# Attention blocks of six, five and five key tiles, with 27 exponential tiles and twelve slots for moving operands

## The chip, the cores and the metric

The kernel runs on one core of a Trainium2 chip. The metric is the device time of one execution in microseconds (us). Its engines work side by side, each through its own queue in order: TensorE (PE, with its weight loads as PEld), VectorE (DVE), ScalarE (ACT), GpSimd (POOL) and SyncE (SP, which issues all DMAs here).

## What is computed

Two independent results stand side by side in the output of 2048 x 2048 values, all in float32. The left half is multi-head attention with 32 heads of width 32 over 2048 rows; the right half is the real part of a two-dimensional Fourier transform, as products with given matrices.

```python
qkv = (x @ wqkv).reshape(B, S, 3, H, Dh)            # S = 2048, D = 1024, H = 32, Dh = 32
scores = einsum("bhqd,bhkd->bhqk", q, k) * Dh ** -0.5
p = softmax(scores, axis=-1)
left = einsum("bhqk,bhkd->bhqd", p, v).reshape(B, S, D) @ wo

a = einsum("bsd,ed->bse", xb, dft_hid_re);  b = einsum("bsd,ed->bse", xb, dft_hid_im)
right = dft_seq_re @ a - dft_seq_im @ b
```

## The kernel before

**Dense products.** The projection to Q, K and V (`qkv`), the two stages of the transform (`dense1`, `dense2`) and the output projection (`project`) are products of large matrices. Each is done as seven products of quarter matrices and sums of quarters instead of eight products, so each stage goes through seven steps (`ORDER`; `STEPS` in `qkv`, where they are split into twelve). Float32 accuracy comes from splitting every operand into a high and a low part and adding three matmuls, so a term of `group` (line 347) is three matmuls of 128x512 at line 357, 12 or 24 of them to a group. These are called fills: 6720 in all, in a fixed order.

**Operands.** A stationary operand (`piece`, line 452) has three buffers for each half. A moving operand (`moving`, line 478) is fetched through a ring of raw tiles (`fetch`, line 383: DMAs, and sums at line 421), then split by `halves` (line 435): a cast to the high part (line 443 on DVE, line 441 on ACT where `spare` allows), and a subtraction for the low part (line 446, on POOL or DVE). The two halves go into one numbered slot of 4 KB for each partition. A step uses eight moving operands, and each slot's split waits until the last fill that used the slot's former content is done. `load_x`, `load_b` and `load_ab` put the operands of even steps into one set of eight slots and those of odd steps into another; the loads of the next step are queued while the step runs, about one after each group. Other slots hold the running sums of the steps (`accs`), and slots 24 to 27 are made in a pool that takes the place of the attention's tiles when these are released (`op_pool`).

**Attention.** For each head three streams of PE work are written out. S (line 1148): scores of 128 query rows against 1024 keys in a PSUM tile `psS` (two buffers), whose maximum DVE takes (line 1154) and whose exponentials ACT sums (line 1157). T (line 1271): the scores transposed, 128 keys by 512 query columns in `psT` (two buffers), shifted by the maxima; ACT writes their exponentials into a tile `pt` (line 1275), of which there are `NPT` = 19. V: after every `PVB` = 4 key tiles, that is 16 `pt` tiles, one block of products with V (line 1289). These use the array as four groups of 32 columns, one for each 512 query columns:

```python
for k, j, box, _, _ in todo:
    nc.tensor.matmul(
        po["p"][j * DH : j * DH + DH, :], VT[h][:, k, :], box["t"], start=(k == t + 1 - PVB), stop=(k == t),
        tile_position=(0, j * DH),
    )
v = op("PE", SWITCH + PVB * PV, pv, [load[t // PVB], *(x[3] for x in todo)], [vuse, *(x[4] for x in todo)])
```

The block's sum leaves PSUM by a copy (line 1300) or an addition (line 1302) on DVE. In the trace each of these V matmuls in plain float32 has two records.

**The order.** A planner (`Plan` and the loop from line 1348) plays the program through with costs written by hand (line 305) and so fixes the order of every engine when the program is built. PE takes S and T as ACT and DVE need them, V blocks when they are ready, and fills in between. Fills are paced by `nf / (FILL - RES) <= done / ATT` (line 1401), where `done` is the planned cost of the attention work begun and `ATT` its total.

**The end.** `behind` (line 1010) is called at the last step (13) of `dense2`: from there raw tiles come from the pool that replaces the attention's, gated by the stores of all heads' results (`over`), and casts may go to ACT (`spare`). `project` loads its first operands through the earlier ring (line 1079), the others through the new one.

Of the kernel before, what the change touches and what calls it, by code (L numbers as in the profile page):

```python
# [19 lines left out]
H = 32  # L20
DH = 32
# [3 lines left out]
NPT = 19  # L25
NE = 4
PVB = 4
# [182 lines left out]
def kernel(  # L210
# [94 lines left out]
    MM, PV, SWITCH, TINY = 0.234, 0.762, 0.62, 0.17  # L305
# [17 lines left out]
    ATT = H * (128 * MM + 16 * PV + 16 / PVB * SWITCH)  # L323
# [41 lines left out]
    slots = [[] for _ in range(28)]  # L365
# [169 lines left out]
    def qkv():  # L535
# [211 lines left out]
        def qk_group(x, W, b, n):  # L747
            p = STEPS[x][0]
            early = x < 5
            h = FIRST.get(p)  # L750
            if p == 1 and n == 0:
                if early:
                    X[2 * b], X[2 * b + 1] = acc(b)
                else:
                    X[2 * b], X[2 * b + 1] = accs(16 + b - PAIRS)
            group(((chunk(W, c), (XS[x, 4 * n + c], whole)) for c in range(4)), 4,
                  gather(p, 2 * b + n, qk_result(b + 8 * h[0], 2 * h[1] + n, early) if h else None, early, None if b % 2 else SCALE))
# [8 lines left out]
        for x, (p, blocks, v) in enumerate(STEPS[:10]):  # L766
            spare[0] = x < 5
            for i, b in enumerate(blocks):
# [8 lines left out]
                if x == 0 and i == 1:  # L777
                    for k in range(4, 8):
                        load_x(0, k)
# [4 lines left out]
                if x == 0:  # L784
                    if i == 1:
                        for c in range(4):
                            load_v_weight(0, c)
                else:
                    for k in range(8 * i // len(blocks), 8 * (i + 1) // len(blocks)):
                        load_x(x + 1, k)  # L790
            for t in range(8 if v else 0):
# [8 lines left out]
            if x == 4:  # L800
                for u in ahead[0].users:
                    att_gate.extend(u)
# [3 lines left out]
        for x in (10, 11):  # L806
            for t in range(8):
                v_group(x, t)
                if x == 10:
                    load_x(11, t)  # L810
                    if t < 4:
                        load_v_weight(11, t)
# [76 lines left out]
    def dense1():  # L889
# [31 lines left out]
        for n in range(8):  # L921
            load_b(0, n)
        X = {}
        for x, p in enumerate(ORDER):
            for i in range(8):
                a = piece(a_terms(p, i), (s1_d[i], s1[i]) if p == 6 else None)
                if p == 1:
                    X[i] = accs(i)
# [7 lines left out]
                if x < 6:  # L936
                    load_b(x + 1, i)
                else:
                    load_ab(0, i)
# [4 lines left out]
    def load_ab(step, k):  # L944
# [11 lines left out]
        AB[step, k] = moving((16 if step % 2 else 8) + k, terms, (t2_d[m][k], t2[m][k]) if p == 6 else None)  # L956

    def dense2():

        y_st = [[[], []] for _ in range(NS)]  # L960
        for m in range(2):
# [13 lines left out]
            for x, p in enumerate(ORDER):  # L975
                step = 7 * m + x
                if step == 13:
                    behind()
                for i in range(8):
                    if p in (1, 7) and i % 2 == 0:  # L980
                        X[p, i // 2] = accs((0 if p == 1 else 4) + i // 2)
# [15 lines left out]
                    if step < 13:  # L997
                        load_ab(step + 1, i)
# [11 lines left out]
    def behind():  # L1010

        over.extend(o for h in o_st for o in h)
        for i in range(24, 28):
# [4 lines left out]
    over, within = [], where[0]  # L1018

    def project():  # L1020
# [15 lines left out]
        def b_terms(p, c):  # L1036
# [11 lines left out]
            1: ([8, 12], 0), 7: ([16, 20], 24), 2: ([0, 16], 12), 6: ([20, 0], 24),  # L1048
            5: ([16, 20], 12), 3: ([0, 16], 24), 4: ([20, 0], 12),
# [29 lines left out]
        tail, where[0] = where[0], within  # L1079
        load_b(1)  # L1080
        load_a(1, J0 + J1)
        where[0] = tail
        for x, p in enumerate(ORDER):
            for i in range(8):
                j, t = divmod(i, 4)
                if p == 1 and i % 2 == 0:
                    X[i // 2] = accs(4 + i // 2)
                if p == 7 and i % 2 == 0:
                    Y[i // 2] = accs(8 + i // 2)
# [168 lines left out]
    def transposed(h):  # L1258
# [4 lines left out]
        for t in range(NS):  # L1263
# [19 lines left out]
            if (t + 1) % PVB == 0:  # L1283
                load, vuse = vts[h]

                def pv(todo=todo, t=t):
                    po["p"] = psD.tile([P, NB], F32, name="pd")
                    for k, j, box, _, _ in todo:
                        nc.tensor.matmul(  # L1289
                            po["p"][j * DH : j * DH + DH, :], VT[h][:, k, :], box["t"], start=(k == t + 1 - PVB), stop=(k == t),  # L1290
# [6 lines left out]
                def gather_o(t=t):  # L1297
                    if t + 1 == PVB:
# [5 lines left out]
                e = op("DVE", EVAC, gather_o, [v] + (oold if t + 1 == PVB else []), [ouse], -1)  # L1304
# [33 lines left out]
    dense2()  # L1338
    project()
# [118 lines left out]
```

## Time and profile before

| | |
|---|---|
| median of three runs | 3033.72 us (3032.64 to 3034.45) |
| profiled execution | 3032.8 us, of which the profile's span is 3031.0 us |
| PE busy | 3004.3 us (99%) |
| DVE busy | 2451.4 us (81%) |
| ACT busy | 2297.5 us (76%) |
| POOL busy | 788.6 us (26%) |
| V matmul records at line 1289 | 4096, first at 268.7 us, last at 2798.3 us |
| TensorE clock granted | 1.000 |

The page of the profile gives busy time by engine, forty slices of the span, the chain of work that ended last, and groups of instructions by line. The timeline lists instructions in order of time, equal ones merged: the start, the length from the first start to the last end, the engine, the line and the tiles. Since matmuls are pipelined, an instruction's length overlaps with the next; what one costs is read from start to start.

### The profile page before, as it was taken

To read this page: it belongs to the slowest core of one execution; us is meant where nothing else is said; L and a number is where in the kernel's file an instruction comes from. 1 tells how busy PE (TensorE), PEld (TensorE's weight loads), DVE (VectorE), ACT (ScalarE), POOL (GpSimd) and SP (SyncE) were. 2 spreads that over 40 slices of the span, in tenths; PEclk is the share of its full clock that TensorE was granted. 3 is DMA by queue.
4 is the path that set the end of the run, shared out by engine and by line. 5 is a ranking of instruction groups with operands and counts; after the bars stand their busy time and mean duration, and the time that the engine had idled before them with its cause. 6 is when DMAs were issued, how large, how long until landed. Compare 5 with 4: busy or idle time off the path is not lost.

```text
span 3031.0 us, 45312 instructions
## 1 busy us (share of the span) xinstructions
PE 3004.3 (99%) x14912; PEld 2142.4 (71%) x14912; DVE 2451.4 (81%) x3303; ACT 2297.5 (76%) x4328; POOL 788.6 (26%) x587
## 2 busy tenths in 40 slices
PE   8999999999999999999999999999999999999999
PEld 7887666666766667666677766676666766666787
DVE  7779888788978878887778888878777888886886
ACT  4347888888888888888888888888888888884321
POOL 2313324222212221221011243332111344221232
PEclk9999999999999999999999999999999999999999
DMA  9975657766635535564534675455433577446942
GB/s 341 351 233 180 192 182 226 222 208 229 227 98 170 175 119 157 156 193 123 156 112 128 198 240 181 147 161 174 132 119 94 167 230 227 150 139 216 372 141 98
DMA packets 376314, 558.07 MB, mean 184 GB/s; under 512 B 110896, under 2 KB 110896, under 8 KB 376016
## 3 DMA queue, kind: packets, MB, share of 16 engines
q1 hardware_dynamic: 376080, 555.17, 57.4%
q8 instruction: 120, 1.97, 0.3%
q14 instruction: 114, 0.93, 0.1%
HBM read 401.93 MB, written 153.09 MB: 183 GB/s over the span
## 4 chain that ended last, share of the span: by engine, by line
PE 90%; DVE 6%; DMA 2%; issue 1%; ACT 1%; SPq 0%; POOL 0%; DVEq 0%; ACTq 0%; POOLq 0%
PE pd L357 39%; PE psT L1271 15%; PE psS L1148 15%; PE pd L1289 15%; PE psT L357 6%; DVE negm L1154 2%; ACT psS L1157 1%; DVE slot L443 1%; DVE h L443 0%; DVE slot L446 0%; DVE l L446 0%; DVE raw L421 0%; DMA er<-in_xa 0%; DVE e L446 0%; DMA raw<-in_wv 0%
## 5 line engine op out<-in xcount | busy, mean ns | idle before, releaser
L1275 ACT ACTIVATE pt<-psT 128x512 f32<-128x512 f32 x2048 | 1167.9, 639 | 352.6 <-PE psT L1271 344.2
L1154 DVE TENSOR_REDUCE negm<-psS 128x1 f32<-128x1024 f32 x1024 | 1237.7, 1220 | 179.8 <-PE psS L1148 173.6
L1157 ACT ACTIVATE psS<-psS,negm 128x1024 f32<-128x1024 f32 x1024 | 1161.1, 1134 | 82.8 <-DVE negm L1154 79.4
L357 PE MATMUL pd<-slot,h 128*128 128x512 f32 x3304 | 1130.7, 394 | 0.1
L1271 PE MATMUL psT<-qs,ks 98*128 98x512 f32 x2048 | 816.5, 403 | 2.0 <-ACT pt L1275 1.5
L357 PEld LDWEIGHTS pd<-slot,h 128*128 128x128 f32 x3304 | 624.8, 189 | 140.7 <-issue 1.7
L357 PE MATMUL pd<-slot,l 128*128 128x512 f32 x1652 | 650.3, 394 | 0.8 <-DVE l L446 0.8
L1271 PEld LDWEIGHTS psT<-qs,ks 98*128 98x128 f32 x2048 | 383.3, 189 | 202.1 <-issue 87.2
L1148 PE MATMUL psS<-ks,qs 96*128 96x512 f32 x1552 | 476.7, 396 | 7.9 <-ACT psS L1157 5.8
L1289 PE MATMUL pd<-pt,vt 128*32 128x512 f32 x4096 | 466.0, 595 | 1.8 <-DVE e L590 0.4
L446 POOL TENSOR_TENSOR l<-raw,h 128x512 fp32r<-128x512 f32 x149 | 199.4, 1338 | 920.8 <-PE psT L1271 425.2
L421 POOL TENSOR_TENSOR raw<-raw,g 128x512 f32<-128x512 f32 x199 | 264.8, 1336 | 504.2 <-DMA raw<-in_ct 115.5
L357 PEld LDWEIGHTS pd<-slot,l 128*128 128x128 f32 x1652 | 312.5, 189 | 70.6 <-DVE l L446 1.1
L1148 PEld LDWEIGHTS psS<-ks,qs 96*128 96x128 f32 x1552 | 290.0, 189 | 83.2 <-ACT psS L1157 18.2
L1289 PEld LDWEIGHTS pd<-pt,vt 128*32 128x32 f32 x4096 | 120.0, 109 | 276.9 <-issue 256.3
L446 POOL TENSOR_TENSOR slot<-raw,slot 128x512 fp32r<-128x512 f32 x129 | 180.2, 1405 | 360.0 <-DVE slot L443 261.8
L1157 ACT ACTIVATION_READ_ACCUMULATOR psS<-psS,negm 128x1 f32 x1024 | 257.4, 251 | 0.0
L357 PE MATMUL pd<-slot,slot 128*128 128x512 f32 x768 | 195.5, 392 | 0.0
L1302 DVE TENSOR_TENSOR ot<-ot,pd 128x512 f32<-128x512 f32 x96 | 65.9, 687 | 157.6 <-PE pd L1289 157.6
L357 PEld LDWEIGHTS pd<-slot,slot 128*128 128x128 f32 x768 | 144.5, 188 | 31.5
L1148 PE MATMUL psS<-ks,qx 96*128 96x512 f32 x496 | 152.1, 397 | 1.4 <-ACT psS L1157 1.4
L443 DVE CAST h<-raw 128x512 fp32r<-128x512 f32 x305 | 138.8, 457 | 15.9 <-PE pd L357 14.9
(117 smaller groups left out, 2002.2 us busy)
## 6 DMA issues: line engine op xcount, KB each, us to landing
raw<-in_ct SPq DMA_DIRECT2D x224, 256.0 KB
g<-in_ct SPq DMA_DIRECT2D x128, 256.0 KB
qk_d<-e SPq DMA_DIRECT2D x52, 512.0 KB
qs<-qk_d SPq DMA_DIRECT2D x128, 192.0 KB
ks<-qk_d SPq DMA_DIRECT2D x128, 192.0 KB
raw<-ab_d SPq DMA_DIRECT2D x96, 256.0 KB
c<-u_d SPq DMA_DIRECT2D x88, 256.0 KB
g<-ab_d SPq DMA_DIRECT2D x80, 256.0 KB
```

What stands on the lines that cost most here:

```text
L357: nc.tensor.matmul(box["ps"], a[1]((a[0].hi, a[0].lo)[u]()), b[1]((b[0].hi, b[0].lo)[v]()), start=k == 0, stop=k == n - 1)
L421: (nc.gpsimd if e == "POOL" else nc.vector).tensor_tensor(out=dest(), in0=dest() if a is None else a.get(), in1=other["q"] if "q" in other ...
L443: nc.vector.tensor_copy(hi(), raw())
L446: (nc.gpsimd if e == "POOL" else nc.vector).tensor_tensor(out=lo(), in0=raw(), in1=f(hi()), op=ALU.subtract)
L1148: nc.tensor.matmul(p[:, i * NB : i * NB + NB], (qx["t"] if own else QS[h % 2][0:96])[:, qt * P : qt * P + P], KS[h % 2][0:96, c * 1024 + i ...
L1154: nc.vector.tensor_reduce(out=ST["negm"][:, c, qt : qt + 1], in_=box["p"], axis=AX.X, op=ALU.max, negate=True)
L1157: nc.scalar.activation(box["p"], box["p"], AF.Exp, bias=ST["negm"][:, c, qt : qt + 1], accum_out=ST["sums"][:, c, qt : qt + 1])
L1271: nc.tensor.matmul(box["p"], KS[h % 2][0:98, t * P : t * P + P], QS[h % 2][0:98, j * NB : j * NB + NB], start=True, stop=True)
L1275: nc.scalar.activation(box["t"], box["p"], AF.Exp)
L1289: nc.tensor.matmul(po["p"][j * DH : j * DH + DH, :], VT[h][:, k, :], box["t"], start=(k == t + 1 - PVB), stop=(k == t), tile_position=(0, ...
L1302: nc.vector.tensor_tensor(out=po["o"], in0=po["o"], in1=po["p"], op=ALU.add)
```

## The change

- V blocks end after key tiles 6, 11 and 16 of a head (`ENDS`), three for each head instead of four. A block waits for all V tiles up to its last, and for its 24 or 20 exponential tiles.
- `NPT` rises from 19 to 27, which takes 16 KB more of each partition.
- Slots 20 to 23 leave the common pool. Moving operands go round in twelve slots: a step's first four operands are queued during the step before, the last four with the step's own first group. Their slots are those of the first four operands of the step before.
- Sums move to the slots left (`SUMS`), and the V weights of two early steps to slots 28 to 31 in the early pool `vp`; the attention's gate waits for their users too.
- `behind` is called after `dense2`, and the first operands of `project` go through its ring too.
- The planner's costs become `PV` = 0.786 and `SWITCH` = 0.515, with three switches for each head in `ATT`.

```diff
-NPT = 19
+NPT = 27
-PVB = 4
+ENDS = (0, 6, 11, 16)
...
-        if i >= 24:
-            return op_pool().tile(shape, dt, name=f"slot{i}")
+        if i >= 20:
+            return (vp if i >= 28 else op_pool()).tile(shape, dt, name=f"slot{i}")
...
+    AROUND, SUMS = (16, 17, 18, 19, 4, 5, 6, 7, 8, 9, 10, 11), (0, 1, 2, 3, 12, 13, 14, 15)
-    MM, PV, SWITCH, TINY = 0.234, 0.762, 0.62, 0.17
+    MM, PV, SWITCH, TINY = 0.234, 0.786, 0.515, 0.17
-    ATT = H * (128 * MM + 16 * PV + 16 / PVB * SWITCH)
+    ATT = H * (128 * MM + 16 * PV + 3 * SWITCH)
...
-            XS[x, k] = moving(8 * ((x + 1) % 2) + k, x_terms(p, k, x >= 5), (tx_d[k], tx[k]) if x == 3 else (t1x_d[k], t1x[k]) if x == 2 else None)
+            if x < 5:
+                i = 8 * ((x + 1) % 2) + k
+            else:
+                i = (8 * (x - 5) + k) % 12 if x < 11 or k < 4 else 8 + k
+            XS[x, k] = moving(i, x_terms(p, k, x >= 5), (tx_d[k], tx[k]) if x == 3 else (t1x_d[k], t1x[k]) if x == 2 else None)
-            WV[x, c] = moving((20 if x in (1, 3, 10) else 16) + c, w_terms(p, lambda i, j: wv[i, 4 * j + c], sv_d[c], sv[c]), (sv_d[c], sv[c]) if p == 6 else None)
+            WV[x, c] = moving((28 if x in (1, 3) else 12 if x == 10 else 16) + c, w_terms(p, lambda i, j: wv[i, 4 * j + c], sv_d[c], sv[c]), (sv_d[c], sv[c]) if p == 6 else None)
...
-            B[x][n] = moving(16 - 8 * (x % 2) + n, b_terms(p, n), (t1_d[n], t1[n]) if p == 6 else None)
+            B[x][n] = moving(AROUND[(8 * x + n) % 12], b_terms(p, n), (t1_d[n], t1[n]) if p == 6 else None)
+                if i == 0:
+                    for n in range(4, 8):
+                        load_b(x, n)
-                if x < 6:
-                    load_b(x + 1, i)
-                else:
-                    load_ab(0, i)
+                if i % 2:
+                    load_b(x + 1, i // 2) if x < 6 else load_ab(0, i // 2)
...
-        AB[step, k] = moving((16 if step % 2 else 8) + k, terms, (t2_d[m][k], t2[m][k]) if p == 6 else None)
+        AB[step, k] = moving(AROUND[(8 * (7 + step) + k) % 12], terms, (t2_d[m][k], t2[m][k]) if p == 6 else None)
-                if step == 13:
-                    behind()
+                            if i == 0 and k:
+                                for c in range(4, 8):
+                                    load_ab(step, c)
-                    if step < 13:
-                        load_ab(step + 1, i)
+                    if step < 13 and i % 2:
+                        load_ab(step + 1, i // 2)
...
-        for i in range(24, 28):
+        for i in range(20, 28):
-        tail, where[0] = where[0], within
         load_b(1)
         load_a(1, J0 + J1)
-        where[0] = tail
...
-            if (t + 1) % PVB == 0:
+            if t + 1 in ENDS:
+                t0 = ENDS[ENDS.index(t + 1) - 1]
-                v = op("PE", SWITCH + PVB * PV, pv, [load[t // PVB], *(x[3] for x in todo)], [vuse, *(x[4] for x in todo)])
+                v = op("PE", SWITCH + (t + 1 - t0) * PV, pv, [*load[: t // 4 + 1], *(x[3] for x in todo)], [vuse, *(x[4] for x in todo)])
...
     dense2()
+    behind()
     project()
```

More of the change, by code (lines that the diff above doesn't have):

```diff
@@ L364 @@
     RAW, HR, LR, GR, ER = Ring(5), Ring(3), Ring(3), Ring(3), Ring(NE)
-    slots = [[] for _ in range(28)]
+    slots = [[] for _ in range(32)]
     def take_slot(i):
@@ L800, in qkv @@
             if x == 4:
-                for u in ahead[0].users:
+                for u in ahead[0].users + slots[28:]:
                     att_gate.extend(u)
@@ L808, in qkv @@
                 v_group(x, t)
[L809 to L812, printed above, removed]
+                if x == 11 and t < 4:
+                    load_x(11, 4 + t)
+                elif x == 10 and t < 2:
+                    for k in range(2):
+                        load_x(10, 4 + 2 * t + k)
+                elif x == 10 and 2 <= t < 6:
+                    load_x(11, t - 2)
+                    load_v_weight(11, t - 2)
         for b in range(8):
@@ L917, in load_b @@
             p = ORDER[x]
[L918 removed]
+            B[x][n] = moving(AROUND[(8 * x + n) % 12], b_terms(p, n), (t1_d[n], t1[n]) if p == 6 else None)
         B = [[None] * 8 for _ in ORDER]
[L921 removed]
+        for n in range(4):
             load_b(0, n)
@@ L1016, in behind @@
         spare[0] = True
-    over, within = [], where[0]
+    over = []
     def project():
```

32 lines of the change are left out of this document (17 added, 15 removed).

## The prediction

> **What bounds the kernel now.** The page comes first: busy time, the slices with the clock, and the chain that ended last.
>
> ```profile
> span 3031.0 us, 45312 instructions
> ...
> PE 3004.3 (99%) x14912; PEld 2142.4 (71%) x14912; DVE 2451.4 (81%) x3303; ACT 2297.5 (76%) x4328; POOL 788.6 (26%) x587
> ...
> PEclk9999999999999999999999999999999999999999
> ...
> PE 90%; DVE 6%; DMA 2%; issue 1%; ACT 1%; SPq 0%; POOL 0%; DVEq 0%; ACTq 0%; POOLq 0%
> ```
>
> TensorE is busy for 99% of the span at an undisturbed clock, and nine tenths of the last chain are its own. A busy PE need not be an efficient one, so the second question is what its time buys, and there the group of the V blocks is to be read beside its neighbours on the other engines.
>
> ```profile
> L1275 ACT ACTIVATE pt<-psT 128x512 f32<-128x512 f32 x2048 | 1167.9, 639 | 352.6 <-PE psT L1271 344.2
> L1154 DVE TENSOR_REDUCE negm<-psS 128x1 f32<-128x1024 f32 x1024 | 1237.7, 1220 | 179.8 <-PE psS L1148 173.6
> ...
> L1289 PE MATMUL pd<-pt,vt 128*32 128x512 f32 x4096 | 466.0, 595 | 1.8 <-DVE e L590 0.4
> ...
> L1302 DVE TENSOR_TENSOR ot<-ot,pd 128x512 f32<-128x512 f32 x96 | 65.9, 687 | 157.6 <-PE pd L1289 157.6
> ```
>
> ACT and DVE wait for PE (344.2 and 173.6 us in these rows), hardly the other way: PE stood 1.8 us in all ahead of V matmuls. The table of stages shows how much room the others have in the attention:
>
> ```profile
> 250.00:2700.00 2450.00, 2438.48 (x12363) 1693.09 (x12363) 2009.68 (x2671) 2080.69 (x3954) 650.99 (x489) 1.00 0.55 171
> ```
>
> The columns are PE, weight loads, DVE, ACT and POOL, then clock, DMA share and GB/s. PE misses 11.5 of 2450 us; DVE is busy for 82% and ACT for 85%. So what shortens PE's own work shortens the kernel, as long as operands still arrive.
>
> **The change part by part. First, the blocks.** What does a block of V cost beyond its products? The timeline of two blocks, one in the middle and the last one, tells it from start to start.
>
> ```profile
> 913.38 0.39 PE L1271 MATMUL psT<-qs,ks 98*128 98x512 f32 x1
> 913.70 3.64 PE L1289 MATMUL pd<-pt,vt 128*32 128x512 f32 x32
> 917.27 0.50 PE L1271 MATMUL psT<-qs,ks 98*128 98x512 f32 x1
> 917.61 0.63 PE L1148 MATMUL psS<-ks,qs 96*128 96x512 f32 x2
> 918.08 0.40 PE L1271 MATMUL psT<-qs,ks 98*128 98x512 f32 x1
> ```
>
> ```profile
> 2794.97 0.39 PE L357 MATMUL pd<-slot,l 128*128 128x512 f32 x1
> 2795.29 3.64 PE L1289 MATMUL pd<-pt,vt 128*32 128x512 f32 x32
> ...
> 2795.74 0.13 PEld L1289 LDWEIGHTS pd<-pt,vt 128*32 128x32 f32 x4 [0.30 <-issue]
> ...
> 2797.89 0.13 PEld L1289 LDWEIGHTS pd<-pt,vt 128*32 128x32 f32 x4 [0.30 <-issue]
> 2798.86 0.50 PE L357 MATMUL pd<-slot,h 128*128 128x512 f32 x1
> ...
> 2799.20 0.40 PE L357 MATMUL psT<-slot,h 128*128 128x512 f32 x1
> ```
>
> The 32 records of a block are eight rounds of four column groups. The weight loads give the rounds' period: six sets of four stand from 2795.74 to 2797.89, five intervals, so 0.43 us to a round and 0.86 us to a key tile. This is throughput, and a longer block keeps it. Around the rounds lies the rest. From the matmul ahead to the second one behind it is 4.23 us in both blocks (917.61 - 913.38, 2799.20 - 2794.97). Two plain matmuls belong to that stretch; two such starts lie 0.47 us apart at 917.61 and 918.08, so 0.23 each. That leaves 4.23 - 0.46 = 3.77 for the block; eight rounds are 8 x 0.43 = 3.44. So **0.33 us is a price per block**: 0.09 on entry, 0.13 after the last round, 0.11 behind the first matmul afterwards.
>
> The change makes three blocks of a head's four, with the same 32 rounds: 32 heads x 1 block x 0.33 = **10.6 us less** on PE. Below it could be nothing, if the 0.33 grew with the block's length; above, the most is what surrounds the rounds plus the last round itself, 0.33 + 0.43 = 0.76, or 24 us, which needs a last round that costs nothing. I take the 0.33 as fixed, since all of it lies outside the rounds. The page "TensorEngine Tiling (Array Packing)" of the Trainium skill (Tiling Modes, Key Properties) says that a change of tiling mode drains the array, which ties the price to the two changes of mode. With the constant of a warm single matmul in "TensorE: Matmul & The Clock Gate" (Single matmul latency), 398 cycles at 2.4 GHz, two drains would be an estimated 0.33 us and the sum 10.6 us as well; the trace agrees for blocks of four, and no row shows a longer one.
>
> DVE loses 32 additions like those of line 1302, 32 x 0.687 = 22 us. They are off the path (they wait for PE), so they count nothing, but they loosen the engine on which the second part leans. A longer block makes ACT and DVE wait longer; that is a rival below. The block's new waits, on 20 or 24 exponentials and on all V tiles so far, sit in PE's queue with fills behind them; the 1.8 us of the L1289 row is the nearest price, and three tiles stay spare as now (19 - 16, 27 - 24), so I take nothing more.
>
> **Second, the slots.** In the built order of before, at least 106 fills lie between the last fill on a slot's old content and the first on its new one. In the changed order 96 refills, 24 sets of four, have only 34 fills, and 34 to 103 PE matmuls of all kinds: at 0.23 us, 11.5 us or more for 23 sets, and 7.8 us for the last, which falls after the attention. Into that time goes the split, whose rows are:
>
> ```profile
> L446 POOL TENSOR_TENSOR slot<-raw,slot 128x512 fp32r<-128x512 f32 x129 | 180.2, 1405 | 360.0 <-DVE slot L443 261.8
> ...
> L443 DVE CAST slot<-raw 128x512 fp32r<-128x512 f32 x230 | 123.6, 544 | 4.8 <-DMA raw<-ab_d 2.6 <-DMA raw<-in_xa 1.7
> ...
> L446 DVE TENSOR_TENSOR slot<-raw,slot 128x512 fp32r<-128x512 f32 x155 | 112.8, 733 | 4.0 <-ACT slot L441 1.5
> ```
>
> Four casts are 4 x 0.544 = 2.2 us of DVE; of four subtractions about half go to each engine (155 and 129), 2 x 0.733 = 1.5 us on DVE and 2 x 1.405 = 2.8 us on POOL. So 3.7 us of DVE beside 2.8 of POOL must fit into 11.5 us or more. They need not be finished at once: the first operand is needed first, the fourth some 9 fills later. The raw data is fetched ahead in its ring; the bytes are the same. I take 1 us in all; ends are 0 and the rival's price.
>
> **Third, the end.** The page's chain and the timeline show one stall behind the attention, where new raw tiles and reloaded sums for the last steps came late:
>
> ```profile
> 2820.75 0.39 PE L357 MATMUL pd<-slot,h 128*128 128x512 f32 x1
> 2822.19 0.50 PE L357 MATMUL psT<-slot,h 128*128 128x512 f32 x1 [1.05 <-DVE h L443]
> 2823.65 0.50 PE L357 MATMUL psT<-slot,l 128*128 128x512 f32 x1 [0.96 <-POOL l L446]
> ```
>
> ```profile
> 2800.00:2830.00 30.00, 27.99 (x123) 22.62 (x122) 24.80 (x44) 3.68 (x6) 3.11 (x3) 1.00 0.96 332
> ```
>
> Two gaps of 1.45 us where 0.23 is due: 2.4 us, with the DMA engines at 96% and 332 GB/s. Step 13 now isn't gated there, so this crowd thins; in exchange `project` may load its first twelve operands only after the last head is stored. The order has 883 fills behind the last block (985 before), 211 of them not `project`'s: 211 x 0.227 = 48 us of cover by the rate of the tail (24 fills in 5.44 us, next row), against 12 x 256 KB = 3.1 MB at 332 GB/s, 9.5 us, plus the way of the last head's result into memory.
>
> ```profile
> 2963.80 5.44 PE pd L357 x24
> ```
>
> With that cover gone it would cost those 9.5 us once. Step 13's casts lose ACT's help, with 7.8 us for one tight set; DVE has no maxima there. I take nothing for the end, between -2.4 and +9.5.
>
> The start and what leads up to the first T matmul are as good as unmoved: 1041 PE matmuls ahead of it, 1042 before. The other slot numbers change no work.
>
> **The sum.** The profiled execution took 3032.8 us (span 3031.0, 1.8 around it), 0.9 under the median of 3033.7. 3032.8 - 10.6 + 1 = 3023.2; forecast **3023**.
>
> **The rivals.** *Late splits (slower).* DVE's 3303 instructions stand in the trace in the order in which they were built. If a cast stands ahead of a maximum and its slot isn't free, maximum, exponential and next score wait too, and a late low part stops a fill, behind which PE's written order waits. Place: the 24 sets. Price: at 82%, DVE has 0.18 x 11.5 = 2.1 us free in the shortest common window, and 3.7 are wanted: 1.6 us late; at every set 24 x 1.6 = 38 us, so 3061. It eats the gain from 10.6 / 24 = 0.44 us a set, and makes the kernel slower by over 0.2% from (10.6 + 6.1) / 24 = 0.7 us. For it: turnover times from 106 fills down to 34. Against it: the 82% contain these casts already, most sets have some 86 matmuls or 20 us, and the order was laid out with the slots' release known. "TensorE: Matmul & The Clock Gate" (Architectural detail) of the Trainium skill calls DVE and ACT strict FIFO, which is what makes this rival possible; no row here shows a cast holding up a maximum.
>
> *Starved ACT (gain eaten).* During a block no S or T comes. ACT and DVE ran dry in the block at 913.70:
>
> ```profile
> 917.81 1.30 ACT L1275 ACTIVATE pt<-psT 128x512 f32<-128x512 f32 x2 [1.40 <-PE psT L1271]
> ```
>
> ```profile
> PEld psS L1148 <- ACT psS L1157: 24.0, 43, 1.8
> ```
>
> 1.40 us idle in a block of four; one of six is 1.72 longer, one of five 0.86. Per head 4 x 1.40 = 5.6 becomes 3 x 1.40 + 1.72 + 2 x 0.86 = 7.6, 65 us more over 32 heads, of some 369 that ACT has free in the stage (2450 - 2081). If waits of S for ACT grew with it, by 7.6 / 5.6, the 24.0 us would become 33: 9 us, giving 3032. Against it: ACT has the room, and fills stand between.
>
> *No saving.* If the price went with the rounds and not with the block, the time stays at 3033. The blocks do get longer: the built order has 64 runs of five tiles and 32 of six. Against it: nothing but the edges is out of step.
>
> *More saved.* The stall of the end goes (2.4) and with it the 1.8 at V and some of the 24.0 us: 3018.
>
> **Chances.** Forecast, 3019 to 3027: 0.62. More saved, 0.08. Gain eaten by starving or by the price's nature, 3028 to 3039: 0.16. Late splits, above: 0.14. About 0.2%, 6 us, is what a measurement of this kernel can tell from none: faster 0.70, same 0.16, slower 0.14. The range goes from 3016 (into the more-saved case) to 3036 (into the eaten ones), and leaves the late splits out.
>
> **What would show it.** Right: 96 V blocks whose rounds stay at 0.43 and whose stretch is 5.95 us for six tiles and 5.09 for five, neighbours included (4.23 + 4 or 2 rounds); PE idle in the attention's stage near 11.5 us; a tail without stalls. Wrong: gaps ahead of line 357 behind the splits at step changes (late splits); more waiting at `psS` and `psT` behind long blocks (starving); edges that grow with the block.

## The result, and the profile after

The changed kernel takes 3028.85 us, the median of 11 runs (3023.11 to 3032.93); the kernel before takes 3034.2 us in the 11 runs beside it (3032.05 to 3040.02). The ratio is 0.9979, with a 95% interval of 0.9970 to 0.9989: 0.21% faster, about 5.4 us less. The forecast was 10.6 us less for the blocks and about 1 us back. So the direction came out, the forecast time of 3023 did not, and half of the forecast gain is missing. The profiled execution took 3029.23 us, its span 3027.3 us.

Of the page, first the counterparts of the lines shown of before:

```profile
span 3027.3 us, 45365 instructions
...
PE 3002.2 (99%) x14912; PEld 2151.6 (71%) x14912; DVE 2403.0 (79%) x3243; ACT 2279.5 (75%) x4312; POOL 849.6 (28%) x631
...
PEclk9999999999999999999999999999999999999999
...
PE 81%; DVE 3%; ACT 1%; DMA 1%; issue 1%; SPq 0%; DVEq 0%; ACTq 0%
...
L1304 PE MATMUL pd<-pt,vt 128*32 128x512 f32 x4096 | 462.1, 597 | 1.7 <-DVE slot L598 1.2
```

Nothing alarming stands here, and that is the lesson of this page: PE is 2.1 us less busy (3002.2 against 3004.3) and 1.6 us less idle (25.1 against 26.7), where 10.6 us less of work was due. The V row is as good as unchanged, since its records overlap; the clock line is all nines, because a digit stands for 90% or more, and 3 or 7 us at half clock vanish in a slice of 76 us. The three places that hold the answer have to be looked for with finer windows.

**The blocks did what was forecast.** The PE timeline of a block of six key tiles, and of one of five, in the kernel after:

```profile
920.10 0.39 PE L1285 MATMUL psT<-qs,ks 98*128 98x512 f32 x1
920.42 5.36 PE L1304 MATMUL pd<-pt,vt 128*32 128x512 f32 x48
...
926.05 1.09 PE L1162 MATMUL psS<-ks,qs 96*128 96x512 f32 x4
```

```profile
891.77 0.39 PE L361 MATMUL pd<-slot,h 128*128 128x512 f32 x1
...
896.51 0.73 PE L1285 MATMUL psT<-qs,ks 98*128 98x512 f32 x2
897.08 1.10 PE L1162 MATMUL psS<-ks,qx 96*128 96x512 f32 x4
```

Six tiles: 926.05 - 920.10 = 5.95 us. Five tiles have two T matmuls behind the block, so one start of 0.23 comes off: 897.08 - 0.23 - 891.77 = 5.08. Over all blocks the medians are 5.953 us (32 blocks) and 5.091 us (64 blocks), beside 4.230 us for the 128 blocks of before. Per head that is 5.953 + 2 x 5.091 = 16.135 instead of 16.920, but one block fewer also leaves two plain matmuls (0.46) standing elsewhere: 0.785 - 0.46 = 0.33, times 32 = 10.4 us less.

**Two stretches without fills.** The PE timeline of after at two places, 720 us apart. Line 1162 issues S, line 1285 T, line 361 a fill; the brackets give the idle time ahead and who ended it.

```profile
1718.87 0.40 PE L1285 MATMUL psT<-qs,ks 98*128 98x512 f32 x1
1719.77 0.73 PE L1162 MATMUL psS<-ks,qs 96*128 96x512 f32 x2 [0.50 <-ACT psS L1171]
1720.33 0.90 PE L1285 MATMUL psT<-qs,ks 98*128 98x512 f32 x2
1721.84 0.73 PE L1162 MATMUL psS<-ks,qs 96*128 96x512 f32 x2 [0.60 <-ACT psS L1171]
1722.41 0.90 PE L1285 MATMUL psT<-qs,ks 98*128 98x512 f32 x2
1723.91 1.03 PE L1162 MATMUL psS<-ks,qs 96*128 96x512 f32 x2 [0.60 <-ACT psS L1171]
...
1725.29 6.46 PE L1304 MATMUL pd<-pt,vt 128*32 128x512 f32 x48
```

```profile
2441.04 0.39 PE L361 MATMUL pd<-slot,h 128*128 128x512 f32 x1
2441.77 0.73 PE L1162 MATMUL psS<-ks,qs 96*128 96x512 f32 x2 [0.34 <-ACT psS L1171]
...
2443.84 0.79 PE L1162 MATMUL psS<-ks,qs 96*128 96x512 f32 x2 [0.60 <-ACT psS L1171]
...
2445.91 1.22 PE L1162 MATMUL psS<-ks,qs 96*128 96x512 f32 x2 [0.30 <-ACT psS L1171]
...
2447.91 4.39 PE L1304 MATMUL pd<-pt,vt 128*32 128x512 f32 x24
```

No fill stands between 1718.87 and the block, nor between 2441.04 and the block. S and T alone go no faster than ACT takes their exponentials: S comes every 2.07 us (1719.77, 1721.84, 1723.91). Then the block of six, for which half a clock shows: 6.46 us at line 1304 instead of 5.36. Windows as long as the disturbance, PE alone, show why. The columns are the window and its length, PE busy and its records, the granted clock, the DMA share and GB/s:

```profile
1120.00:1123.40 3.40, 1.71 (x7) 1.00 0.63 184
1123.40:1126.80 3.40, 3.40 (x9) 0.50 0.70 219
1720.80:1724.20 3.40, 2.20 (x6) 0.99 0.87 260
1724.20:1727.60 3.40, 3.40 (x15) 0.50 0.76 240
2441.00:2444.40 3.40, 2.46 (x8) 1.00 1.03 310
2444.40:2447.80 3.40, 3.10 (x7) 0.50 1.05 383
2447.80:2451.20 3.40, 3.40 (x17) 0.50 0.78 246
```

A window in which PE has only 6 to 8 matmuls, where 15 fit at 0.23 us, is followed by one window at half clock, or two when the next is thin as well. Four such windows are 13.65 us, and PE is busy for almost all of it, so about 6.7 us are lost. That also says how PE's busy time hides the loss: 10.4 us less of work and 6.7 us more of slowness would make 3.7 us less; it fell by 2.1. The other 1.6 us are not explained here.

What the two stretches cost in all can be read from start to start. The first should take 12 matmuls x 0.23 = 2.8 us from 1718.87 to 1725.29 and takes 6.4; the remaining 2.3 us at half clock lose 1.15 more: 4.8 us. The second has 13 matmuls, 3.0 us, and takes 6.9 from 2441.04 to 2447.91; 3.3 us at half clock behind it lose 1.65: 5.5 us. Together **10.3 us, as much as the blocks save**. The third place, at 1122 us, has fills around it; S waited there 1.69 us for ACT and the half clock cost 1.7. Idle time ahead of S adds to 1.70, 1.24 and 1.69 us at the three places, 4.6 in all, while PE's idle time as a whole fell by 1.6; so 6.2 us less of it stands elsewhere, 2.0 of them in the stall of before at 2822 us. That is where the gain that is left comes from. The 10.3 us are counted against a PE that never waits, and before waits for ACT too, in smaller pieces. The rows of PE's own waits in before and in after (sum, times, longest):

```profile
PE psS L1148 <- ACT psS L1157: 7.2, 14, 1.4
```

```profile
PE psS L1162 <- ACT psS L1171: 9.5, 16, 1.7
```

So against before the waiting grew by 2.3 us, and the clock, with 6.7 us, is the larger loss. In sum the spans of the two profiles should differ by 10.4 - 6.7 + 1.6 = 5.3 us; they differ by 3.7.

**Why the stretches have no fills.** Both fall in the steps of `dense2` with p = 6, one for each half, after the group's twelfth fill, and at a moment when a fill isn't there yet the planner writes S and T only. A moving operand of that step is a sum of three quarters, three loads and two additions through a ring of five raw tiles (line 409) and one of three for second operands (line 418). Before, all eight were loaded during the step ahead. Now the step's first group queues four of them, and ahead of its own second stationary piece, which has three terms as well. `dense1` has a three-term step too, but there the four operands are queued behind the piece, and no such stretch follows: apart from the two, the longest run without a fill in the attention of after is nine S and T matmuls and a block, as in before. Below are the issues on SP's queue and one addition on POOL, in the timeline of after:

```profile
2430.93 0.45 SPq L418 DMA_DIRECT2D g<-ab_d  x1
...
2444.66 0.33 SPq L418 DMA_DIRECT2D g<-in_ct  x1
```

```profile
2443.36 1.28 POOL L425 TENSOR_TENSOR raw<-raw,g 128x512 f32<-128x512 f32 x1 [2.08 <-DMA g<-in_ct]
```

Seven second operands leave from 2430.93 to 2444.66, 1.2 to 4.1 us apart, which fits three buffers that come free one by one; the piece's own loads of `in_ct` stand behind the four operands' `ab_d`, and POOL waits for them, 2.08 us here, just when PE has no fill. At this place the DMA engines are full as well (1.03 and 1.05 in the windows above, against 0.87 and 0.76 at the first), so how much of the delay is the rings and how much the transfers is not settled.

### The profile page after: what moved, and what is told of

The parts are those of the page before. It is cut to its first block, busy times and chain, and to the rows that moved or that the text cites. A ratio compares the mean times of both kernels' runs of the same rounds, so it can differ in the third digit from the quotient of the medians.

```text
span 3027.3 us, 45365 instructions
## 1 busy us (share of the span) xinstructions
PE 3002.2 (99%) x14912; PEld 2151.6 (71%) x14912; DVE 2403.0 (79%) x3243; ACT 2279.5 (75%) x4312; POOL 849.6 (28%) x631
## 4 chain that ended last, share of the span: by engine, by line
PE 81%; DVE 3%; ACT 1%; DMA 1%; issue 1%; SPq 0%; DVEq 0%; ACTq 0%
PE pd L361 36%; PE psT L1285 15%; PE pd L1304 14%; PE psS L1162 14%; PE psT L361 3%; DVE negm L1168 1%; ACT psS L1171 1%; DVE raw L425 0%; DVE h L447 0%; DMA raw<-o_d 0%; DVE slot L447 0%; ACT pt L1289 0%; DMA out<-e 0%; DMA c<-u_d 0%; DMA g<-in_wd 0%
## 5 line engine op out<-in xcount | busy, mean ns | idle before, releaser
L1171 ACT ACTIVATE psS<-psS,negm 128x1024 f32<-128x1024 f32 x1024 | 1174.3, 1147 | 77.2 <-DVE negm L1168 73.2
L361 PE MATMUL pd<-slot,h 128*128 128x512 f32 x3352 | 1152.7, 394 | 0.0
L361 PEld LDWEIGHTS pd<-slot,h 128*128 128x128 f32 x3352 | 634.2, 189 | 141.9 <-issue 0.8
L361 PE MATMUL pd<-slot,l 128*128 128x512 f32 x1676 | 660.2, 394 | 0.5 <-DVE l L450 0.5
L425 POOL TENSOR_TENSOR raw<-raw,g 128x512 f32<-128x512 f32 x214 | 285.8, 1341 | 469.8 <-DMA raw<-in_ct 115.8
L450 POOL TENSOR_TENSOR slot<-raw,slot 128x512 fp32r<-128x512 f32 x145 | 203.4, 1410 | 368.6 <-DVE slot L447 232.7
L1171 ACT ACTIVATION_READ_ACCUMULATOR psS<-psS,negm 128x1 f32 x1024 | 270.8, 264 | 0.0
L447 DVE CAST h<-raw 128x512 fp32r<-128x512 f32 x321 | 153.2, 478 | 15.7 <-PE pd L361 13.5
L425 DVE TENSOR_TENSOR raw<-raw,g 128x512 f32<-128x512 f32 x158 | 121.8, 776 | 33.2 <-DMA raw<-in_ct 9.8
```

What stands on the lines that cost most here:

```text
L361: nc.tensor.matmul(box["ps"], a[1]((a[0].hi, a[0].lo)[u]()), b[1]((b[0].hi, b[0].lo)[v]()), start=k == 0, stop=k == n - 1)
L425: (nc.gpsimd if e == "POOL" else nc.vector).tensor_tensor(out=dest(), in0=dest() if a is None else a.get(), in1=other["q"] if "q" in other ...
L447: nc.vector.tensor_copy(hi(), raw())
L450: (nc.gpsimd if e == "POOL" else nc.vector).tensor_tensor(out=lo(), in0=raw(), in1=f(hi()), op=ALU.subtract)
L1171: nc.scalar.activation(box["p"], box["p"], AF.Exp, bias=ST["negm"][:, c, qt : qt + 1], accum_out=ST["sums"][:, c, qt : qt + 1])
```

## The experiments

The theory under test: the blocks save their 10.6 us, and most of it is lost again in the two stretches without fills, through waiting for ACT and then through the clock. Rivals: twelve slots cost something at every refill (late splits); or the long blocks themselves make ACT starve or the clock drop. Where a kernel's time is given as a ratio, it is against the kernel before on the same chip.

**The same kernel once more** (`again`), without an edit.

> The changed kernel once more, unchanged, for another profile. Theory: the waits for ACT in the two fill-less stretches near 1719 and 2441 us come again, since the order is fixed; the half-clock intervals need not, since the windows in which the clock is set fall otherwise: 0 to 14 us of half clock, each interval behind a window in which TensorE was idle for over half, time 3023 to 3033. Rival two: half clock behind long V blocks without idle ahead.

3027.13 us in one run. Its windows at the three places, PE alone:

```profile
1710.00:1730.00 20.00, 18.67 (x88) 0.83 0.82 268
2435.00:2455.00 20.00, 18.74 (x88) 0.83 0.94 316
1113.00:1127.00 14.00, 12.22 (x53) 1.00 0.67 222
```

Both stretches come back with idle time and half clock (0.83 over 20 us is 6.8 us at half). The third place has its wait, 1.78 us at 1119.27, but keeps its clock. So the stretches belong to the order of the program. At the third place the clock did not follow: counted in steps of 3.413 us from this run's first half clock, the wait lies within one window, 1115.85 to 1119.26, in which PE is busy for 1.64 us with 8 matmuls; in after it was 1.71 us with 7. Why the one cost clock and the other did not is not shown.

**Score matmuls issued again where no fill is there** (`hot`, and the same kernel once more as `hot2`). S is issued twice and T four times where the planner finds no fill ready: 28 more matmuls, the same results. They stand where PE would wait for ACT.

```diff
-                for i in range(2):
+                for i in range(4 if twice[0] else 2):
+                    i %= 2
...
+                    for _ in range(4 if twice[0] else 1):
...
+            twice[0] = n in "ST" and pl.now > 300 and nf < len(fills) and (fills[nf][0].left > 0 or fills[nf][0].ready > pl.now + 1.0)
+            if twice[0]:
+                o.cost += (2 if n == "S" else 3) * MM
```

> The changed kernel, but where the planner finds no fill near, the scores' matmuls are issued twice (S) or four times (T) with the same operands into the same tile; results stay the same. So TensorE is kept active in the two fill-less stretches, while operands, slots and V blocks stay as late and as long. Theory (half clock follows idle TensorE): no half-clock time at the two stretches, at most 3.4 us elsewhere, and the time falls by about the 5 us that 10.2 us at half clock cost: 3024 us. Rival two (long V blocks bring the clock down): half-clock time stays 7 us or more, time 3029 or more.

> The changed kernel with doubled score matmuls once more, unchanged, beside these two: 3022.6 us within 2, clock 1.000, ratio 0.997 against before.

3022.55 us (3020.84 to 3025.66), ratio 0.9968 (0.9956 to 0.9979); the second time 3023.95 us, ratio 0.9965 (0.9952 to 0.9979). The granted clock is 1.000 in all these runs. PE's timeline and windows of `hot` at the same places:

```profile
1716.33 1.09 PE L1164 MATMUL psS<-ks,qs 96*128 96x512 f32 x4
1717.26 2.02 PE L1288 MATMUL psT<-qs,ks 98*128 98x512 f32 x8
```

```profile
1710.00:1730.00 20.00, 20.00 (x112) 1.00 0.82 276
2435.00:2455.00 20.00, 19.97 (x110) 1.00 0.80 272
```

The planner counts the repeated matmuls, so it also spreads the rest of the order differently, and the waits for ACT go from the stretch. With every long block and every slot refill of the change in place, this kernel is 10 to 11 us faster than before, which is what the blocks alone promised: that speaks against both rivals. Against the profile of before PE is 4.6 us less busy (10.4 less for the blocks, 6.4 more for the 28 matmuls at 0.23) and 7.8 us less idle. It doesn't split the 10 us into waiting and clock, and the order moved with the edit.

**The kernel before, starved at the same two fills** (`before_starved`). Blocks of four, sixteen slots; at fills 3756 and 5100 the order holds the fills back until 13 steps of S and T are written.

```diff
+    alone = {3756: 13, 5100: 13}
...
+        hold = nf in alone and alone[nf] > 0
-        if nf < len(fills):
+        if nf < len(fills) and not hold:
...
+            if hold and n in "ST":
+                alone[nf] -= 1
```

> The kernel before (sixteen slots, blocks of four, 19 exponential tiles), but the planner holds the fills back at two places, fill 3756 and fill 5100, until 13 S and T steps are written: 18 score matmuls and then a block of four with no fill, as in the changed kernel at the same two fills. Theory (fill-less stretches make TensorE wait for ACT, and half clock follows that idle time): some 2.3 us of waiting in each, half-clock intervals of 3.4 or 6.8 us right behind both in most executions, granted clock 0.997 to 0.999, time 3039 to 3044 us, while its plain runs stay at clock 1.000 and 3033.6. Rival two (it takes long V blocks): clock stays 1.000 and the time rises by the waiting alone, to 3038 at most.

3042.74 us (3040.0 to 3048.42), ratio 1.0029 (1.0019 to 1.0039): some 8.8 us more, for two stretches. Windows of PE at the first of them:

```profile
1774.10:1777.50 3.40, 1.22 (x6) 1.00 0.77 249
1777.50:1780.90 3.40, 3.40 (x10) 0.50 1.04 298
```

A thin window gives half clock here too, with no block of more than four tiles: long blocks aren't needed for it. (A stall of 2.9 us at 2830 us is in this time as well; before has two of 1.45 us behind its attention, so it adds nothing to the difference.)

**Blocks of four with all the rest of the change** (`blocks4`).

```diff
-ENDS = (0, 6, 11, 16)
+ENDS = (0, 4, 8, 12, 16)
...
-    ATT = H * (128 * MM + 16 * PV + 3 * SWITCH)
+    ATT = H * (128 * MM + 16 * PV + 4 * SWITCH)
```

> The changed kernel with twelve slots and 27 exponential tiles, but V blocks of four key tiles again; its built order has no fill-less stretch. Theory (0.33 us a block, and no loss from the slots but in fill-less stretches): 128 blocks with a stretch of 4.23 us, time 3033 to 3035, ratio 1.000 against before. Rival one (tight refills cost everywhere, some 5 to 7 us): 3039 to 3041. If the blocks saved nothing: 3029, as the changed kernel.

3045.78 us (3043.22 to 3047.6), ratio 1.0043 (1.0030 to 1.0055). That is a miss by 10 us and more. The blocks themselves have a median of 4.229 us, as before the change, so the price per block stands; most of the excess lies behind the attention: stalls of 3.9 us (up to 2835.22) and 2.5 us, two smaller ones, and 6.8 us at half clock from 2834.4 on. The time of this kernel is therefore no clean measure of the block price; its trace is. It was the first sign that the end, taken as 0, is a place of its own.

**Two of the four late operands behind the stationary piece, in all steps** (`split`).

```diff
-                                for c in range(4, 8):
+                                for c in range(4, 6):
...
+                            if i == 0 and k:
+                                for c in range(6, 8):
+                                    load_ab(step, c)
```

> The changed kernel, but in each step's first group of the second transform stage only two of the last four moving operands are queued ahead of the group's second stationary piece, the other two behind it. In the built order the two fill-less stretches of the changed kernel (18 score matmuls and a six-tile block with no fill, in the two steps with three-term operands) are gone; blocks and slots stay. Theory (the loss of some 7 us against the 10.6 that the blocks save comes from these two stretches, in which TensorE stands idle for half of the time and then runs at half clock): half-clock time falls from 13.7 us to 3.4 or nothing, stretches of six and five tiles stay 5.95 and 5.09 us, time 3024 us, ratio 0.9967. Rival one (all 24 tight refills cost a little each): two of 24 change, time stays at 3028. Rival two (long V blocks by themselves bring the clock down): 32 blocks of six tiles are still there, half-clock time stays, 3028.

3038.19 us (3032.73 to 3039.98), ratio 1.0014 (1.0005 to 1.0023): a miss. The stretch at 2441 us goes; of the other, a run of ten S and T matmuls is left in the same step, from 1739.00 to 1743.91, with S waiting 0.6 us for ACT twice and a window at half clock. While PE works, its profile has 10.2 us at half clock, where 3.4 or nothing was expected. And the loads of the last steps now meet those of `project`. PE, and then SP's queue, in its tail:

```profile
2824.71 0.39 PE L361 MATMUL psT<-slot,h 128*128 128x512 f32 x1
2827.36 0.50 PE L361 MATMUL psT<-slot,h 128*128 128x512 f32 x1 [2.26 <-DVE slot L447]
```

```profile
2821.11 2.88 SPq L409 DMA_DIRECT2D raw<-in_wo  x1
2824.09 0.38 SPq L409 DMA_DIRECT2D raw<-in_ct  x1
```

One load of `project` (`in_wo`) sits on SP's queue for 2.88 us, where its neighbours take some 0.4, and the transform's next load waits behind it until 2824.09; what held it the trace doesn't say. The fill at 2827.36 doesn't wait for that load, but for a sum and two casts on DVE from 2825.93 on. Their data were issued before, at 2820.14 (`t_d`) and 2820.64 (`in_ct`), and by the trace's semaphores landed only at 2825.86 and 2826.52. So an order of loads that cures one place came with new stalls at another, and this run says nothing for or against the refills.

**The same, in the three-term steps alone** (`split6d`), all four operands behind the piece; and with the repeated score matmuls besides (`hot6d`).

```diff
-                            if i == 0 and k:
+                            if i == 0 and k and p != 6:
...
+                            if i == 0 and k and p == 6:
+                                for c in range(4, 8):
+                                    load_ab(step, c)
```

> The changed kernel, but only in the two steps with three-term operands the last four moving operands are queued behind the first group's second stationary piece. In the built order the long fill-less stretches shrink: 13 score matmuls in the one step, 9 in the other, which the kernel before has fifteen times; 883 fills behind the last block, as in the changed kernel (the kernel that was split at every step had stalls of 2.7 and 1.9 us there). Theory: half-clock time 0 to 7 us, a tail within 2 us of the changed kernel's, time 3024 to 3027 us. If the tail stalls as in the kernel split at every step: 3030 or more, and the stretches are then not what keeps the gain small.

> Both: operands of the three-term steps behind the piece, and score matmuls doubled where the planner finds no fill near. Theory: no half-clock time, stretches of 5.95 and 5.09 us; against the doubled kernel alone (3022.6 us) only the waiting in the fill-less stretches can go, 2 to 4 us: 3019 to 3023 us. If the doubled matmuls were what costs there: 3022.6 or more.

`split6d`: 3027.0 us (3022.6 to 3034.54), ratio 0.9976 (0.9968 to 0.9985), and its runs differ with the clock: 3022.6 to 3028.8 where 1.000 was granted, 3027 and more at 0.999. `hot6d`: 3025.01 us (3021.43 to 3027.96), ratio 0.9965 (0.9951 to 0.9979), above the range expected and no better than `hot`. PE's waits of S for ACT over the whole run, in `split6d` and in `hot`, show where `split6d` gave its gain back:

```profile
PE psS L1165 <- ACT psS L1174: 13.1, 20, 2.2
```

```profile
PE psS L1164 <- ACT psS L1173: 5.6, 10, 1.3
```

The profiled execution of `split6d` had a clock of 1.000 and a span of 3027.0 us, as good as after's: no clock loss, but 3.6 us more of these waits than the 9.5 of after. PE is 4.9 us less busy than in after and 4.6 us more idle. A new order of loads gives the planner a new order of everything.

**A fourth buffer for second operands** (`g4`), paid with one exponential tile and one raw tile at the end.

```diff
-NPT = 27
+NPT = 26
...
-    RAW, HR, LR, GR, ER = Ring(5), Ring(3), Ring(3), Ring(3), Ring(NE)
+    RAW, HR, LR, GR, ER = Ring(5), Ring(3), Ring(3), Ring(4), Ring(NE)
...
-        where[0] = (Ring(9), Ring(5),
+        where[0] = (Ring(8), Ring(5),
```

> The changed kernel with four buffers instead of three for the second operands of sums (line 418's tiles), paid for with one exponential tile (26) and one raw tile at the end (8). Its built order has no stretch of over ten S and T matmuls without a fill; 818 fills behind the last block. Theory (the fill-less stretches come from the three-term operands' loads, twelve of which go through few buffers at the step's start): half-clock time 0 to 3.4 us, time 3021 to 3026 us if the tail's stalls stay near 5 us; with stalls there as in the kernels with the moved end, 3030.

3025.68 us (3022.49 to 3026.39), ratio 0.9968 (0.9957 to 0.9980), as expected. The span of its profile is 3021.5 us. Windows at the stretches:

```profile
1712.00:1730.00 18.00, 16.14 (x62) 0.91 0.89 295
2435.00:2455.00 20.00, 20.00 (x91) 1.00 0.98 318
```

Neither place is a stretch without fills any more. What is left at the first is a wait ahead of one fill, for the high part of a stationary piece, with one window at half clock:

```profile
1715.48 0.51 PE L361 MATMUL pd<-slot,h 128*128 128x512 f32 x1 [1.73 <-DVE h L447]
```

So the ring of three for second operands is one of the links: with one buffer more both stretches go and the piece still comes late at one place. The twelve slots are as they were; the exponential tile, the raw tile and with them the planner's order changed too.

**Both** (`hotg4`): the edits of `hot` and `g4`.

> The kernel with four buffers for second operands, and score matmuls doubled where the planner finds no fill near. Theory: clock 1.000; time 3020 to 3024 us if the tail's stalls stay near 5 us, no better than the doubled kernel (3022.6 us), since the order is already free of long stretches.

3033.68 us (3031.9 to 3036.11), ratio 1.0000 (0.9992 to 1.0009): the clearest miss. No window at half clock stands in its profile while PE works, but PE waits 9.1 us for S's ACT instead of `hot`'s 5.6 or `g4`'s 3.8, and is idle for 27.1 us in all instead of 18.9 or 23.3. Two edits that each gain some 10 us over before gain nothing together, since each builds another order.

**The end as it was before** (`tail_back`): `behind` called at step 13, and `project`'s first operands through the earlier ring.

```diff
+                if step == 13:
+                    behind()
...
+        tail, where[0] = where[0], within
         load_b(1)
         load_a(1, J0 + J1)
+        where[0] = tail
...
-    behind()
```

> The changed kernel with the end as before: the pool that replaces the attention's is used from step 13 on, and the output projection's first operands come through the earlier ring. Its built order has the same two fill-less stretches and the same 883 fills behind the last block. Theory (the move of the end is worth little either way): tail's stalls between 2 and 8 us instead of 5, time 3026 to 3032 us. If the move were what ate the gain: 3023.

3040.08 us (3034.81 to 3042.71), ratio 1.0020 (1.0011 to 1.0028), 11 us above the changed kernel: a miss in size. PE's timeline, and SP's queue, behind the attention:

```profile
2822.62 0.39 PE L361 MATMUL pd<-slot,h 128*128 128x512 f32 x1
2825.56 0.49 PE L361 MATMUL psT<-slot,h 128*128 128x512 f32 x1 [2.55 <-ACT h L445]
...
2830.41 0.63 PE L361 MATMUL psT<-slot,h 128*128 128x512 f32 x1
2835.41 0.80 PE L361 MATMUL psT<-slot,h 128*128 128x512 f32 x1 [4.37 <-ACT h L445]
```

```profile
2820.04 0.32 SPq L1338 DMA_DIRECT2D o_d<-ot  x1
...
2827.47 0.43 SPq L409 DMA_DIRECT2D raw<-t_d  x1
```

With twelve slots, step 13's own second half of operands is loaded in step 13, and with `behind` called there it waits for the gate of the attention's tiles: its four loads of `t_d` leave from 2821.39 to 2827.47, right behind the store of the last head's result at 2820.04. In after they leave from 2797.30 to 2810.65. Two stalls of 2.9 and 5.0 us and some 10 us at half clock follow. Moving the end was not a side edit: without it the change would have lost.

## Why the prediction was right and wrong

**The time: inside the range, for a reason that was not in it.** 3028.85 us missed the forecast band of 3019 to 3027 and fell into the one of 3028 to 3039, which was given 0.16 for starving or for a price that grows with the block. Neither came true. That the range of 3016 to 3036 held is owed to its width, 20 us around a saving of 10.6, and so to luck as far as the mechanism goes.

**The blocks: right in every figure.** Stretches of 5.95 and 5.09 us were forecast and 5.953 and 5.091 measured; the rounds stay at 0.43 us and the price at 0.33 us a block whatever its length. The page "TensorEngine Tiling (Array Packing)" of the Trainium skill (Tiling Modes, Key Properties) says that a change of tiling mode drains the array. The blocks of five and six tiles agree with it too, since the price did not grow.

**The slots: the failed step.** "I take 1 us in all" was wrong by the size of the gain: about 10 us. The step weighed what DVE and POOL have to split in a tight set against the time until its fills, and treated all 24 sets alike; it called the bytes the same and the raw data fetched ahead. Two of the 24 sets are unlike the rest, those of the three-term steps of `dense2`, and there it's neither DVE nor the slots but the supply: three loads an operand through a ring of three, queued ahead of the stationary piece that the same group needs. `g4`, with a fourth buffer, has neither stretch. The other 22 cost nothing that shows: `hot` keeps them all and comes out at the block's saving.

The rival of late splits named the right place, the refills, but not the mechanism. PE's written order hardly waited behind a late low part: in the waits of after, one fill in the whole attention and tail waits for a low part, 0.5 us for `l` at line 450. The planner had seen the lateness and written S and T instead; what waits is S, for ACT. A gap "ahead of line 357 behind the splits at step changes", the sign that the prediction gave, would have missed it.

**The clock: not in the prediction.** It read "an undisturbed clock" off one profile, as a property of the kernel, and it was one of its order. Half of the stretches' cost came by that way. All eleven executions of the changed kernel show a granted clock of 0.997 to 0.999. The kernel before is not quite undisturbed either: of the 24 executions beside `before_starved` 15 show 1.000, the others 0.998 or 0.999. The third place, at 1122 us, shows a share of chance in it: the same wait cost clock in one execution and none in the other. The sign that was named for a right forecast, PE idle in the attention's stage near 11.5 us, came nearly true, 2450.00 - 2437.56 = 12.4 us; time at half clock counts as busy, so this sign could not see the loss.

```profile
250.00:2700.00 2450.00, 2437.56 (x12360) 1708.12 (x12362) 1967.74 (x2623) 2054.01 (x3922) 713.77 (x533) 1.00 0.56 174
```

**The end: right in the sum, wrong as a part.** 0 was taken, and the tail was indeed as fast as before (one gap of 0.9 us at 2850). But this 0 is against a kernel with sixteen slots; inside the change the move is worth 11 us. The cover of 211 fills, 48 us, held.

**The rivals.** Starved ACT behind long blocks is not what happened: S waits for ACT 25.8 us instead of 24.0, where 33 had been worked out, and `hot`, with the same blocks, has 18.4. These are rows of weight loads, which wait beside running matmuls, so they were the wrong price: PE's own row was 7.2 us, which the same factor makes 9.8. It became 9.5, but half of that stands at the three places and not behind blocks all over the run. No saving is refuted by the stretches of the blocks. More saved, 3018, is what `hot` comes near, with the clock kept and the stretches full: its fastest run took 3020.84 us.

**What stays open.** Orders with nearly equal work differ by up to 9.3 us in PE's waits of S for ACT (`g4` 3.8, `hot` 5.6, `hotg4` 9.1, `split6d` 13.1); which choice of the planner makes them was not settled. So no run shows the stretches taken out with all else in its place: `split6d` in its profile, and `hotg4`, lose nothing to the clock in the attention, and the one is no faster than after, the other no faster than before. What the stretches cost is read from the trace of after and from `before_starved`, where putting them in cost 8.8 us. The stretches' 10 us were not split into clock and waiting by a run of their own. The best kernels measured are `hot`, 3022.6 and 3024.0 us, and `g4`, 3025.7 us without any added work; the intervals of their ratios touch that of the change.

## What to carry to other kernels

Where buffers are taken away, don't cost the refills at their average: look for the step with the most loads per operand, and for what its queue puts ahead of what is needed first. When a planner fixes the order, late data doesn't show as a wait for that data; look for stretches in which one of the interleaved streams is missing, and see which engine bounds what is left. And when a gain fails to appear though its part is exact, cut the granted clock into windows of a few us before trusting a page that shows nines.

## What the runs showed of the hardware

In after, TensorE's clock falls to half three times. Each time it follows a window of about 3.41 us in which the engine had only 6 to 8 matmuls, where 15 fit, with no idle gap longer than 1.69 us; it lasts 3.41 us, or 6.83 us where PE had gaps at half clock as well (2444.40 to 2447.80, busy for 3.10 us). Not every such window does it: the one of `again` with 8 matmuls did not. In after, half clock starts at 1123.4, 1724.2 and 2444.4 us, 600.8 and 720.2 us apart, which are 176 and 211 times 3.413 us. "TensorE: Matmul & The Clock Gate" of the Trainium skill (Part 1, What's actually happening) gives a window of 3413 ns that runs freely, and two states, half and full; the traces agree with both. The same page of the Trainium skill (Why this matters for your kernels) advises that idle gaps should stay under some 3 us. At the two stretches idle gaps of 0.3 to 0.6 us, repeated, were enough, and the measurement decides.

In `tail_back` a DMA that wasn't ready held SP's queue and all behind it: the store of the last head's result waited 4.3 us for DVE, and no other DMA was issued between 2815.71 and 2820.04 us. In `split` the issue of a single load took 2.88 us, where its neighbours take 0.4, for a reason that the trace doesn't give, and the load behind it left at 2824.09.
